# Single-chunk loads of an expert's second weight into three buffers, and no format conversion in the steps that empty the accumulators

## The chip, the cores and the metric

One core of a Trainium2 chip runs the kernel. The metric is device time in microseconds (us) of one execution, lower being better. The kernel before was run three times: 1201.28, 1201.47 and 1202.61 us, with a median of 1201.47 us.

## The reference, cut to what matters

Attention goes first: 32 packed queries `p` per head attend over `k` and `v`, then the 576 queries `q` attend over that packed result. Its output, 2304 tokens of 512, goes through a mixture of four experts, and that through one wide layer with a rational activation.

```python
p_packed = sm_attn(p, k, v)
x = sm_attn(q, p_packed, p_packed)          # 2304 x 512
for e in range(4):                          # experts: w1[e] 512x1024, w2[e] 1024x512
    h = np.maximum(x @ w1[e], 0.0)
    out += p[:, e:e + 1] * (h @ w2[e])
h = out @ w_in                              # 512x2048
g = (a0 + a1*h + a2*h*h + a3*h*h*h) / (1 + |b0|*|h| + |b1|*h*h + 1e-6)
return g @ w_out                            # 2048x512
```

`w_in` and `w_out` arrive as float64; the kernel turns them into float32 pairs on the chip.

## The kernel before, in words

Every float32 product is made of three products of reduced-precision parts: a high part (a rounded copy) and a low part (value minus high part). The copy is made by ACT, the subtraction by POOL or DVE. So each operand of TensorE (PE) costs an ACT and a POOL instruction as well.

**Units and steps.** The work of the experts is a list `units` (line 430): four experts `e`, four batches `bb`, two halves `a_` of the batch's tokens (288 each), eight chunks `c` of 128 of the 1024 inner columns, 256 units in all (`NUM`). The loop at line 674 takes one step `kk` per unit. In step kk PE computes the first product of unit kk (`emit_h`, line 497, six matmuls of 288 columns, the tile `h`). DVE makes `hw` from it (line 507: relu, times the token's weight `pw`), ACT its high part `hh` (508), POOL its low part `hl` (509). Then PE computes the second product of an earlier unit (`emit_out`, line 579, twelve matmuls into four banks of `acc`); it runs two units behind (`lag`, line 656). With chunk 7 a half is complete, and `emit_acc` empties its four banks: ACT copies them for the first expert (614), DVE adds them to the running sum for the others (616). The next half's chunk 0 starts the banks anew, one step later. With kk counted modulo 8, chunk 7's second product and the emptying stand in the steps where it is 1, and the next chunk 0 in those where it is 2.

**Hand-over from one expert to the next.** The second weight's eight chunks stand split in eight slots of `wp` (tile `w`). When the last half of expert e has used chunk c, `refill` (659) calls `put_w2(e + 1, c)` (119) one step later: ACT copies the chunk from the raw buffer into the slot (122), POOL subtracts (123). That is eight steps in a row, c = 0 to 7, in steps that are 3, 4, 5, 6, 7, 0, 1, 2 modulo 8, and there are three hand-overs, e = 0 to 1, 1 to 2, 2 to 3. Expert 0's chunks are put during the start (lines 415, 416, 463). The raw chunks are loaded by `load_raw2` (114): 512 KB, two chunks, into one buffer `r2`. After the odd chunk, `put_w2` issues the load of the next two (125). The load is on SP's queue, whose instructions go out in order. It waits until POOL has read both chunks of the old pair.

**Format conversion.** `narrowing` (160) is a generator that converts `w_in` and `w_out` in 32 tasks. One task takes seven calls of `next(cvt)`: a load (174), four calls with two DVE instructions each (192 and 193, 196 and 197, 199 and 201, 203 and 204), one call with the split (ACT 210, POOL 211), and one with two stores (214). So four of seven calls carry DVE work. Two buffers alternate. The loop makes one call in an even step and two in an odd one (714), from step 40 on. At step 208 it makes what calls are left (680).

**Order inside a step**, as issued, on every engine: first product and its `hw`, `hh`, `hl`; side work (attention for later batches; in two steps of each 16, blocks of the combined first weight, lines 146, 148 and 135); conversion calls; `put_w2`; second product; emptying of the banks. Each engine and SP's queue run their instructions in that order.

Of the kernel before, what the change touches and what calls it, by code (L numbers as in the profile page):

```python
# [8 lines left out]
F32 = mybir.dt.float32  # L9
# [10 lines left out]
def kernel(ctx, tc, q, k, v, p, probs, w1, w2, w_in, a, b, w_out, out):  # L20
    nc = tc.nc
    B, H, S, D = q.shape
    NT, E = probs.shape
    DM = w1.shape[1]
    F1 = w1.shape[2]
    F2 = w_in.shape[1]
    P = 128
# [12 lines left out]
    NCH1 = F1 // P  # L40
# [11 lines left out]
    rawp = moe.enter_context(tc.tile_pool(name="rawp", bufs=1, side="right"))  # L52
    pwp = moe.enter_context(tc.tile_pool(name="pwp", bufs=2, side="right"))

    def f32(ap):
        return ap.bitcast(F32)

    with tc.manual_schedule():
# [47 lines left out]
        raw2 = {}  # L106
# [3 lines left out]
        def load_raw1(e, fh):  # L110
            raw1[fh] = tl = rawp.tile([P, KC, FH], F32, tag=f"r1{fh}", name="r1")
            nc.sync.dma_start(out=tl, in_=w1[e][:, fh * FH:(fh + 1) * FH].rearrange("(k p) f -> p k f", p=P))

        def load_raw2(e, c):
            if e < E:
                raw2[0] = tl = rawp.tile([P, 2, DM], F32, tag="r2", name="r2")
                nc.sync.dma_start(out=tl, in_=w2[e][c * P:(c + 2) * P, :].rearrange("(k p) f -> p k f", p=P))

        def put_w2(e, c):
            w = wts[e, c] = wp.tile([P, 2, DM], F32R, tag="w", name="w")  # L120
            r = raw2[0][:, c % 2, :]
            nc.scalar.activation(out=w[:, 0, :], in_=r, func=AF.Copy)  # L122
            nc.gpsimd.tensor_tensor(out=w[:, 1, :], in0=r, in1=f32(w[:, 0, :]), op=ALU.subtract)  # L123
            if c % 2 == 1:
                load_raw2(*((e, c + 1) if c + 1 < NCH1 else (e + 1, 0)))

        def put_final(n, j):
            w = wts["f", n, j] = wp.tile([P, 2, DM], F32R, tag="w", name="w")
# [204 lines left out]
        def st_s2(i):  # L333
            d = st[i]
            ps = bank2("s2")
            scores(ps, bd[:, i, :], d["qT"])
            t2 = ap1.tile([P, NBLK, 32], F32, tag="t2", name="t2", bufs=2)
            for hf in range(2):
                nc.vector.transpose(
                    out=t2[:, hf * (NBLK // 2):(hf + 1) * (NBLK // 2), :].rearrange("p a n -> p (a n)"),  # L340
                    in_=ps[:, hf, :HALF])
            d["t2"] = t2
# [48 lines left out]
        st_s1(1)  # L391
        st_ppt(0)
        st_s2(0)
        load_raw2(0, 0)
        load_raw1(0, 1)
        st_tr(1, "qr", 0)
        st_tr(1, "qr", 1)
# [124 lines left out]
        def emit_mid(u):  # L522
            if u[0] == "m":
                return
            m, s, c1, c0 = mid[u]
            emit_c1(u)
            nc.vector.scalar_tensor_tensor(out=m, in0=s, scalar=b_abs[:, 1:2], in1=m, op0=ALU.mult, op1=ALU.add)  # L527
            nc.vector.reciprocal(out=m, in_=m)  # L528

        def emit_end(u):  # L530
            if u[0] == "m":
                return
            m, s, c1, c0 = mid[u]
            hh = hp.tile([P, TOK], F32R, tag="hh", name="hh")
            nc.gpsimd.tensor_tensor(out=m, in0=m, in1=c1, op=ALU.mult)  # L535
            nc.scalar.copy(out=hh, in_=m)  # L536
            hs[u] = (hh, None)

        def emit_c1(u):
            m, s, c1, c0 = mid[u]  # L540
            nc.vector.tensor_tensor(out=c1, in0=s, in1=c1, op=ALU.mult)  # L541
            nc.gpsimd.tensor_tensor(out=c1, in0=c1, in1=c0, op=ALU.add)  # L542

        def emit_low(u):
            if u[0] == "m":
                return
            m = mid.pop(u)[0]
            hh = hs[u][0]
            hl = hp.tile([P, TOK], F32R, tag="hl", name="hl")
            nc.gpsimd.tensor_tensor(out=hl, in0=m, in1=f32(hh), op=ALU.subtract)  # L550
            hs[u] = (hh, hl)

        def emit_last(u, v):

            def tt(o, x, y, op):
                nc.vector.tensor_tensor(out=o, in0=x, in1=y, op=op)

            parts = {}
            for w in (u, v):
                hs[w] = [hp.tile([P, TOK], F32R, tag=nm, name=nm) for nm in ("hh", "hl")]  # L560
                m, s, c1, c0 = mid.pop(w)
                cuts = [slice(0, TOK)] if w == u else [slice(x * P, x * P + P) for x in range(SUB)]
                parts[w] = [[y[:, o] for y in (m, c1, *hs[w])] for o in cuts]
                if w == v:
                    nc.vector.scalar_tensor_tensor(out=m, in0=s, scalar=b_abs[:, 1:2], in1=m, op0=ALU.mult, op1=ALU.add)
                else:
                    tt(m, m, c1, ALU.mult)
                    nc.scalar.copy(out=hs[w][0], in_=m)
            (m, _, hh, hl), = parts[u]
            tt(hl, m, f32(hh), ALU.subtract)  # L570
            for (m, c1, hh, hl) in parts[v]:
                nc.vector.reciprocal(out=m, in_=m)
                tt(m, m, c1, ALU.mult)
                nc.scalar.copy(out=hh, in_=m)  # L574
                tt(hl, m, f32(hh), ALU.subtract)
# [60 lines left out]
        def emit_x2(t, bb, c0, n, o, kc):  # L636
            hi, lo = (x[:, kc:kc + 2, o:o + n] for x in xs[t])
            src = acc[bb][:, kc:kc + 2, c0:c0 + n]
            nc.scalar.copy(out=hi, in_=src)
            nc.gpsimd.tensor_tensor(out=lo, in0=src, in1=f32(hi), op=ALU.subtract)  # L640
# [3 lines left out]
        for t in range(NTILE):  # L644
            r = t * TOK
            while r < (t + 1) * TOK:
                n = min((t + 1) * TOK - r, S - r % S)

                n = min(n, HALF - r % HALF)
# [6 lines left out]
        def lag(n):  # L656
            return 2 if n < NUM - 4 else 3 if n < NUM else LAGF
# [16 lines left out]
        for kk in range(NU + LAGF):  # L674
            if kk == ATT:
                att.close()
                accp2 = ctx.enter_context(tc.tile_pool(name="accp2", bufs=1, reuse_waits="tile"))
                acc += [accp2.tile([P, KC, S], F32, name=f"acc{i}") for i in range(2, B)]
                cvt = narrowing(tail.enter_context(tc.tile_pool(name="cv", bufs=2, reuse_waits="tile")))
            if kk == NUM - 3 * PH:  # L680
                for _ in cvt:
                    pass
                tail.close()
                xp0 = ctx.enter_context(tc.tile_pool(name="xp0", bufs=1, reuse_waits="tile"))
                for t in range(2):
                    xs[t] = [xp0.tile([P, KC, TOK], F32R, name=f"x{nm}{t}") for nm in "HL"]
            if kk == NUM:
                moe.close()
                apt.__exit__(None, None, None)
                ps_y = ctx.enter_context(tc.tile_pool(name="ps_y", bufs=2, space=PSUM, reuse_waits="tile"))  # L690
                tp = ctx.enter_context(tc.tile_pool(name="tp", bufs=3, side="right", reuse_waits="tile"))
                yp = ctx.enter_context(tc.tile_pool(name="yp", bufs=3, side="right", reuse_waits="tile"))
                xp1 = ctx.enter_context(tc.tile_pool(name="xp1", bufs=1, side="right", reuse_waits="tile"))
                for t in range(2, NTILE):
                    xs[t] = [xp1.tile([P, KC, TOK], F32R, name=f"x{nm}{t}") for nm in "HL"]
            two_back = units[kk - 2] if 2 <= kk < NU else ("m",)
            if kk < NU - 2:
                emit_end(two_back)
            if kk < NU:
                emit_h(units[kk])  # L700
            if kk == NU:
                emit_c1(units[-1])
            elif kk >= NU - 2:
                emit_end(two_back)
            for f, args in side.pop((kk, 0), ()):
                f(*args)
            if 1 <= kk < NU:
                emit_mid(units[kk - 1])
            if kk < NU:
                emit_low(two_back)  # L710
            elif kk == NU:
                emit_last(*units[-2:])
            emit_acc()
            for _ in range(2 if kk % 2 else 1):
                next(cvt, None)
            if todo and todo[0][0] <= done_cols[0] and (kk < NUM or kk % 2 == 0) and todo[0][1][0] in xs:
                emit_x2(*todo.pop(0)[1])
            if 1 <= kk <= NU and units[kk - 1][0] == "f":
                refill(units[kk - 1], 0)
            if done > refilled:  # L720
                refill(units[done - 1], 1)
                refilled = done
            while done < NU and done + lag(done) <= kk:
                emit_out(units[done])
                done += 1
                if done <= NUM:
                    emit_acc()
            for f, args in side.pop((kk, 1), ()):
                f(*args)
# [30 lines left out]
```

## Time and profile before

| | |
|---|---|
| median of 3 runs | 1201.47 us |
| profiled execution | 1200.13 us |
| its span, first to last instruction | 1198.4 us |
| PE busy | 1127.1 us (94%) |
| DVE busy | 750.0 us (63%) |
| POOL busy | 625.1 us (52%) |
| ACT busy | 542.1 us (45%) |
| mean granted clock of TensorE | 0.977 |

Busy time is the time in which an engine had an instruction under way. A row of the timeline gives start, duration, engine, line, operation, tiles and a count; in brackets stands how long the engine was idle before it and what it waited for. PE can be busy and still not at its peak, so the pace of the steps says more than the share.

### The profile page before, as it was taken

Reading aid. Unit: us, or ns where it says so; the run is one execution under the profiler, and the core shown is the slowest. Engines: PE = TensorE matmul, PEld = TensorE weight load, DVE = VectorE, ACT = ScalarE, POOL = GpSimd, SP = SyncE. Lnnn points to the kernel's source line nnn. Section 1 sums busy time; section 2 is a strip of 40 time slices with the busy share of each in tenths; the row PEclk is TensorE's granted clock in tenths of the full one; section 3 lists DMA queues with packets and bytes.
Section 4 is the critical chain, followed back from the end, with each engine's and each line's share of the span. In section 5 each row is a group of like instructions: output and inputs, shape, how many; then the busy total and the mean of one; then the engine's idle time right before and its main releaser. Section 6 shows DMA issues by size and latency. Waiting matters only on the chain.

```text
span 1198.4 us, 20491 instructions
## 1 busy us (share of the span) xinstructions
PE 1127.1 (94%) x8081; PEld 1027.5 (86%) x8081; DVE 750.0 (63%) x1052; ACT 542.1 (45%) x1081; POOL 625.1 (52%) x658
## 2 busy tenths in 40 slices
PE   5799999969999979999989999999999999999996
PEld 4478889969999878999979999988998899999995
DVE  2343435646677656676632333287888888889886
ACT  3444433332222222222222322177777877787774
POOL 0553435463444354434363533368787777767773
PEclk8799999989999999999999999999999999999998
DMA  9443214242325233324320000243333633354321
GB/s 250 114 119 85 65 46 145 89 122 94 115 78 184 76 111 111 96 96 150 95 76 6 11 6 11 80 138 131 112 139 106 194 125 122 135 148 157 119 93 53
DMA packets 61391, 125.91 MB, mean 105 GB/s; under 512 B 6768, under 2 KB 28272, under 8 KB 61296
## 3 DMA queue, kind: packets, MB, share of 16 engines
q1 hardware_dynamic: 61296, 124.62, 33.3%
q8 instruction: 63, 1.03, 0.4%
q14 instruction: 32, 0.26, 0.1%
HBM read 103.06 MB, written 21.53 MB: 104 GB/s over the span
## 4 chain that ended last, share of the span: by engine, by line
PE 81%; DVE 5%; POOL 5%; DMA 4%; ACT 2%; issue 2%; SPq 0%; ACTq 0%; DVEq 0%; POOLq 0%
PE acc L579 45%; PE h L497 30%; DMA r<-in_moe_w_dram 3%; PE wb L146 3%; POOL w L123 2%; PE tr L274 2%; POOL hl L509 1%; DMA vr<-in_v_dram 1%; PE s L283 1%; DVE m L528 1%; PE pp L320 1%; DVE hw L507 1%; DVE acc L616 1%; ACT e L296 0%; ACT w L122 0%
## 5 line engine op out<-in xcount | busy, mean ns | idle before, releaser
L579 PE MATMUL acc<-hh,w 128*128 128x288 f32 x2048 | 455.4, 298 | 22.6 <-ACT acc L614 9.0
L509 POOL TENSOR_TENSOR hl<-hw,hh 128x288 fp32r<-128x288 f32 x256 | 210.5, 823 | 367.1 <-ACT hh L508 365.9
L579 PEld LDWEIGHTS acc<-hh,w 128*128 128x128 f32 x2048 | 346.0, 190 | 28.7 <-issue 13.6
L507 DVE SCALAR_TENSOR_TENSOR hw<-h,pw 128x288 f32<-128x288 f32 x256 | 116.6, 456 | 327.6 <-PE h L497 290.8
L579 PE MATMUL acc<-hl,w 128*128 128x288 f32 x1024 | 304.6, 297 | 9.0 <-POOL hl L509 8.9
L508 ACT CAST hh<-hw 128x288 fp32r<-128x288 f32 x256 | 110.5, 432 | 381.9 <-DVE hw L507 381.8
L528 DVE RECIPROCAL m<-m 128x384 f32<-128x384 f32 x95 | 242.6, 2553 | 3.2
L497 PE MATMUL h<-aH,wb 128*128 128x288 f32 x1024 | 219.9, 303 | 5.7 <-DVE wb L135 5.7
L579 PEld LDWEIGHTS acc<-hl,w 128*128 128x128 f32 x1024 | 194.6, 190 | 11.0 <-POOL hl L509 11.0
L497 PE MATMUL h<-xH,w 128*128 128x384 f32 x768 | 197.0, 337 | 3.0 <-DVE m L527 3.0
L497 PEld LDWEIGHTS h<-aH,wb 128*128 128x128 f32 x1024 | 165.0, 191 | 36.5 <-issue 25.7
L579 PE MATMUL acc<-w,hh 128*128 128x512 f32 x576 | 194.9, 393 | 0.2 <-ACT hh L574 0.2
L497 PE MATMUL h<-aL,wb 128*128 128x288 f32 x512 | 152.6, 298 | 0.3 <-POOL aL L372 0.3
L497 PEld LDWEIGHTS h<-xH,w 128*128 128x128 f32 x768 | 140.4, 188 | 13.0 <-DVE m L527 5.4
L535 POOL TENSOR_TENSOR m<-m,c 128x384 f32<-128x384 f32 x94 | 95.8, 1019 | 70.9 <-DVE m L528 70.9
L497 PE MATMUL h<-xL,w 128*128 128x384 f32 x384 | 129.4, 337 | 0.0
L579 PEld LDWEIGHTS acc<-w,hh 128*128 128x128 f32 x576 | 108.1, 188 | 21.5 <-ACT y L622 0.8
L579 PE MATMUL acc<-w,hl 128*128 128x512 f32 x288 | 113.9, 395 | 0.0
L542 POOL TENSOR_TENSOR c<-c,c 128x384 f32<-128x384 f32 x96 | 97.9, 1020 | 6.2 <-DVE c L541 4.1
L550 POOL TENSOR_TENSOR hl<-m,hh 128x384 fp32r<-128x384 f32 x94 | 95.8, 1019 | 8.0 <-ACT hh L536 8.0
L497 PEld LDWEIGHTS h<-aL,wb 128*128 128x128 f32 x512 | 97.6, 191 | 0.7 <-POOL aL L372 0.7
L541 DVE TENSOR_TENSOR c<-h,c 128x384 f32<-128x384 f32 x96 | 52.5, 547 | 51.9 <-ACT h L518 49.2
(92 smaller groups left out, 1264.1 us busy)
## 6 DMA issues: line engine op xcount, KB each, us to landing
w<-nw SPq DMA_DIRECT2D x96, 512.0 KB, 4.2
r<-in_moe_w_dram SPq DMA_DIRECT2D x8, 1024.0 KB, 5.8
r<-in_moe_w_dram SPq DMA_DIRECT2D x16, 512.0 KB, 3.4
raw<-in_moe_w_in_dram SPq DMA_DIRECT2D x16, 512.0 KB, 4.2
raw<-in_moe_w_out_dram SPq DMA_DIRECT2D x16, 512.0 KB, 3.7
nw<-raw SPq DMA_DIRECT2D x32, 256.0 KB, 2.3
nw<-t SPq DMA_DIRECT2D x32, 256.0 KB, 2.8
kr<-in_k_dram SPq DMA_DIRECT2D x8, 576.0 KB, 4.6
```

Of the source, the lines that this page charges most:

```text
L123: nc.gpsimd.tensor_tensor(out=w[:, 1, :], in0=r, in1=f32(w[:, 0, :]), op=ALU.subtract)
L146: nc.tensor.matmul(ps[32 * c:32 * c + 32, g, :], bd[r, 2 * bb + g, 32 * c:32 * c + 32], raw1[fh][r, c, :], start=True, stop=True, tile_pos ...
L497: nc.tensor.matmul(ps[:, :n], w, x, start=(i == 0), stop=(i == len(ops) - 1))
L507: nc.vector.scalar_tensor_tensor(out=hw, in0=ph, scalar=0.0, in1=pw[t], op0=ALU.max, op1=ALU.mult)
L508: nc.scalar.copy(out=hh, in_=hw)
L509: nc.gpsimd.tensor_tensor(out=hl, in0=hw, in1=f32(hh), op=ALU.subtract)
L528: nc.vector.reciprocal(out=m, in_=m)
L535: nc.gpsimd.tensor_tensor(out=m, in0=m, in1=c1, op=ALU.mult)
L541: nc.vector.tensor_tensor(out=c1, in0=s, in1=c1, op=ALU.mult)
L542: nc.gpsimd.tensor_tensor(out=c1, in0=c1, in1=c0, op=ALU.add)
L550: nc.gpsimd.tensor_tensor(out=hl, in0=m, in1=f32(hh), op=ALU.subtract)
L579: nc.tensor.matmul(ps[:, :n], w, x, start=(first and i == 0), stop=(last and i == 2))
```

## The change

`load_raw2` loads one chunk (256 KB) instead of two, into one of three buffers of half the size; it takes a running number n = 8e + c. Three loads are issued at the start. Each `put_w2` of chunk n issues the load of chunk n + 3. The second edit sets how many conversion calls a step makes: none where kk is 1 modulo 8, two in the other odd steps, one in even steps, and two where kk is 4 modulo 8.

```diff
-        def load_raw2(e, c):
-            if e < E:
-                raw2[0] = tl = rawp.tile([P, 2, DM], F32, tag="r2", name="r2")
-                nc.sync.dma_start(out=tl, in_=w2[e][c * P:(c + 2) * P, :].rearrange("(k p) f -> p k f", p=P))
+        def load_raw2(n):
+            if n < E * NCH1:
+                raw2[n] = tl = rawp.tile([P, DM], F32, tag="r2", name="r2", bufs=3)
+                nc.sync.dma_start(out=tl, in_=w2[n // NCH1][n % NCH1 * P:(n % NCH1 + 1) * P, :])
 
         def put_w2(e, c):
+            n = e * NCH1 + c
             w = wts[e, c] = wp.tile([P, 2, DM], F32R, tag="w", name="w")
-            r = raw2[0][:, c % 2, :]
+            r = raw2.pop(n)
             nc.scalar.activation(out=w[:, 0, :], in_=r, func=AF.Copy)
             nc.gpsimd.tensor_tensor(out=w[:, 1, :], in0=r, in1=f32(w[:, 0, :]), op=ALU.subtract)
-            if c % 2 == 1:
-                load_raw2(*((e, c + 1) if c + 1 < NCH1 else (e + 1, 0)))
+            load_raw2(n + 3)
...
-        load_raw2(0, 0)
+        for n in range(3):
+            load_raw2(n)
         load_raw1(0, 1)
...
-            for _ in range(2 if kk % 2 else 1):
+
+            for _ in range(0 if kk % NCH1 == 1 else 2 if kk % 2 else 1 + (kk % NCH1 == 4)):
                 next(cvt, None)
```

## Rows read from the trace of the kernel before

**Rows 1.** Waits of PE over the span: us in total, times, longest us.

```profile
PE acc L579 <- ACT acc L614: 9.0, 1, 9.0
PE acc L579 <- DVE acc L616: 8.9, 9, 1.8
PE acc L579 <- POOL hl L509: 8.9, 8, 1.4
```

**Rows 2.** Busy time by engine in two stretches of 16 steps.

```profile
core 0: us, PE busy (x) PEld busy (x) DVE busy (x) ACT busy (x) POOL busy (x), PEclk, DMA share, GB/s
332.88:373.30 40.42, 40.42 (x328) 38.42 (x320) 27.30 (x51) 11.09 (x22) 18.22 (x20) 1.00 0.40 125
687.98:728.40 40.42, 40.42 (x328) 38.42 (x320) 12.61 (x26) 9.37 (x19) 14.20 (x18) 1.00 0.03 8
```

**Rows 3.** Timeline of PE: first matmul of six steps, all at the same place modulo 16.

```profile
238.25 0.40 PE L497 MATMUL h<-aH,wb 128*128 128x288 f32 x1
...
290.29 0.40 PE L497 MATMUL h<-aH,wb 128*128 128x288 f32 x1
...
416.77 0.40 PE L497 MATMUL h<-aH,wb 128*128 128x288 f32 x1
...
470.85 0.40 PE L497 MATMUL h<-aH,wb 128*128 128x288 f32 x1
...
597.12 0.40 PE L497 MATMUL h<-aH,wb 128*128 128x288 f32 x1
...
647.55 0.40 PE L497 MATMUL h<-aH,wb 128*128 128x288 f32 x1
```

**Rows 4.** Chain that ended last, 244 to 268 us: start, us, what.

```profile
252.66 3.44 DMA r<-in_moe_w_dram
...
256.18 0.64 ACT w L122
...
256.89 1.27 POOL w L123
...
260.15 4.14 DMA r<-in_moe_w_dram
```

**Rows 5.** Timeline of PE at the end of the first hand-over.

```profile
265.34 0.61 PE L579 MATMUL acc<-hh,w 128*128 128x288 f32 x1 [9.02 <-ACT acc L614]
```

**Rows 6.** Timeline at one emptying of the banks by DVE.

```profile
391.58 0.69 DVE L204 TENSOR_TENSOR u<-u,t 128x512 f32<-128x512 f32 x1
392.19 1.18 DVE L616 TENSOR_TENSOR acc<-acc,acc 128x288 f32<-128x288 f32 x3
```

**Rows 7.** Timeline of an undisturbed step and the start of the next.

```profile
240.73 0.43 PE L497 MATMUL h<-aH,wb 128*128 128x288 f32 x2
...
242.80 1.09 POOL L509 TENSOR_TENSOR hl<-hw,hh 128x288 fp32r<-128x288 f32 x1 [0.33 <-ACT hh L508]
...
243.11 0.43 PE L497 MATMUL h<-aH,wb 128*128 128x288 f32 x2
```

**Rows 8.** DMA issues: KB each, median us from issue to landing.

```profile
nw<-raw SPq DMA_DIRECT2D x32, 256.0 KB, 2.3
```

**Rows 9.** Groups by line on POOL: busy us, mean ns, idle before.

```profile
L509 POOL TENSOR_TENSOR hl<-hw,hh 128x288 fp32r<-128x288 f32 x256 | 210.5, 823 | 367.1 <-ACT hh L508 365.9 <-DMA nw<-raw 0.5
...
L123 POOL TENSOR_TENSOR w<-r,w 128x512 fp32r<-128x512 f32 x32 | 41.9, 1313 | 32.7 <-ACT w L122 32.7
```

**Rows 10.** Timeline of POOL and DVE early in the second hand-over.

```profile
421.76 1.29 POOL L211 TENSOR_TENSOR t<-u,raw 128x512 fp32r<-128x512 f32 x1 [2.02 <-ACT raw L210]
...
423.07 1.52 DVE L192 TENSOR_SCALAR u<-raw 128x512 int32<-128x512 int32 x1
...
425.21 1.47 POOL L123 TENSOR_TENSOR w<-r,w 128x512 fp32r<-128x512 f32 x1
```

**Rows 11.** Timeline at the start: the first weight blocks, on PE and ACT.

```profile
32.94 1.10 PE L146 MATMUL wb<-r,bd 64*32 64x512 f32 x8
...
36.66 0.99 ACT L148 CAST wb<-wb 128x1024 fp32r<-128x1024 f32 x1
```

**Rows 12.** Waits of SP's queue: us in total, times, longest us.

```profile
SPq L117 <- POOL w L123: 69.0, 15, 11.9
```

## The prediction

> **What bounds the kernel now.** The table shows PE busy for 94% of the span, so I first asked what PE waits for. The list of waits [rows 1] names three that touch this change, and each is some 9 us: once for ACT's copy out of the banks, nine times for DVE's emptying of the banks, eight times for POOL's low part `hl`. A wait understates its harm (the engine starts up again, and the clock may have gone down), so I priced by the pace of the steps.
>
> The pace of undisturbed work comes from two stretches of 16 steps without a hand-over [rows 2]: 40.42 us with format conversions running and 40.42 us without. So conversions cost PE nothing there. Against this stand the stretches between first matmuls at the same place modulo 16 [rows 3]. The three hand-overs lie in 238.25 to 290.29, 416.77 to 470.85 and 597.12 to 647.55: 52.04, 54.08 and 50.43 us, that is 11.6, 13.7 and 10.0 us too long, 35.3 us together. The two stretches between them hold 48 steps each and take 126.48 and 126.27 us against 121.26, so 5.2 and 5.0 us too long, 10.2 us together; the drain waits of [rows 1] are what lies in them. All that this change can give back is these 45.5 us, since before 238 us and after 648 us PE shows no wait for an emptying, and no hand-over lies there.
>
> What makes a hand-over long is seen in the chain [rows 4]: a load of two chunks takes 3.44 us, ACT's copy 0.64, POOL's two subtractions (1.27 for one) with a unit's `hl` between them the rest, and only then does the next load go out, 7.49 us after the last one, that is 3.75 us per chunk. PE frees a slot each step, and a step is 2.38 us [rows 7]. The load is late, and ACT, in order, stands in its queue at the copy of a chunk that hasn't landed; behind it wait `hh` of the current units and, at the end of the first hand-over, the emptying of the banks, for which PE sits idle for 9.02 us [rows 5]. That the weights themselves are not yet due is no help: it is ACT's queue that is blocked.
>
> What makes a drain long is seen in one row pair [rows 6]: conversion work (the last piece 0.69 us) stands ahead of the four additions in DVE's queue, in the very step in which PE needs the banks next.
>
> **The change part by part.**
>
> *Chunk loads, three buffers.* At a hand-over's start three chunks lie ready. Load n + 3 goes out when POOL has done with chunk n, and is wanted three steps, 7.1 us, later. A 256 KB transfer landed in 2.3 us [rows 8] (that is a store; a load of 512 KB took 3.44 to 4.14 [rows 4]). Even with 4.14 us and the 1.9 us of copy and subtraction it is there 1 us early. So ACT's wait for the landing goes. What is late next is POOL. In the eight steps of a hand-over it has eight `hl` of 0.823 us and eight subtractions of 1.313 [rows 9], 17.1 us, and one or two splits of 1.29 us [rows 10] from the conversions: 18.4 to 19.7 us, against 8 x 2.38 = 19.0 us of PE. POOL may lag: `hl` of the step at 240.73 ended at 243.89, and it is read after 245.49, the start of the step after next [rows 7], so 1.6 us are free. By the mean rows nothing is left over. With every instruction at its disturbed length (1.47 for the subtraction [rows 10], 1.09 for `hl` [rows 7]) POOL needs 20.5 + 2.6 = 23.1 us, and 2.5 us per hand-over stay. The means already hold the disturbances as they came, so I keep 1 us each, 3.0 in all, between 0 and 7.5. Gain 32.3 us.
>
> *SP's queue.* It gets 16 more issues and 16 more waits for POOL. Behind a waiting load stand the row `pw` for the half after this one (due eight steps later), conversion loads and stores, and loads of the first weight, due a phase later. A wait ends within the chunk's own step, and nothing behind it is due sooner than that. Cost 0; if the cover were gone, it is the rival on the slower side.
>
> *The start.* 768 KB instead of 512 KB go out ahead of the second half of expert 0's first weight. Half of a 3.44 us load [rows 4] bounds the delay: 0 to 1.7 us. The blocks made of that weight are multiplied from 32.94 us, and ACT copies them at 36.66 [rows 11], as it is busy with other work; most of the delay is hidden there. I take 0.3.
>
> *Conversions moved.* Steps that are 1 modulo 8 lose two calls, steps that are 4 gain one: 11 calls in eight steps instead of 12. From step 40 to 208 there are 21 such rounds, 231 calls, and 1 + 32 x 7 = 225 are needed; so the work is still done in time, about 14 steps later than before, and step 208 finds none to catch up. Each call takes along its loads, stores, ACT copy and POOL split; they keep their order. In the emptying step DVE now has `hw` and the additions alone, and the drains go. A last piece from the call in the step before (two operations of 0.69 [rows 6]) can still stand ahead, but a step earlier. I keep 0.7 of 10.2 us, between 0 and 3. Gain 9.5 us.
>
> What the moved calls could cost: steps 3, 4, 5 modulo 8 now make two calls each. The conversions' DVE time is 27.30 - 12.61 = 14.7 us in 24 calls [rows 2], so a whole task of seven is 4.3 us. Six calls hold at most that, and the `hw` and the block subtraction beside them are 12.61 us in 16 steps, 2.4 us in three. 6.7 us in 7.1 us: no lag, cost 0, and lag of 1.6 us is free besides.
>
> *Sum.* 1200.13 - 32.3 + 0.3 - 9.5 = 1158.6 us for the profiled execution. This lies 1.3 us under the median of the runs, 1201.47, so I forecast **1159.9 us**.
>
> **The rivals.** 0.2% of this time, 2.4 us, is about what a measurement of this kernel can tell from no change.
>
> *Half of the hand-over stays* (0.14). POOL and DVE get in each other's way: a DVE conversion took 1.52 us while POOL subtracted [rows 10]. The Trainium skill ("SBUF — State Buffer", "Who interferes with whom") says that such pairs exclude each other for a whole instruction, whichever starts first; the trace agrees, with that 1.52 us. With POOL full for 19 us, DVE is slowed all through, `hw` and so `hh` come late, and ACT's order passes it on. For it: POOL stands at the edge by the sum above. Against: in the stretch with conversions [rows 2] DVE was busy for 27.30 of 40.42 us, with room left. Price: half of 35.3, 17.6 us instead of 3.0, which gives 1174.5 us.
>
> *The drains stay in part* (0.07): the call in the step before, or the one at 0 modulo 8, runs over. Half of 10.2 us stays, and the time is 1159.9 + 4.4 = 1164.3 us.
>
> *The loads come one at a time* (0.03), the slower side. SP's order decides: if something ahead of load n + 3 holds SP for more than three steps, 7.1 us, after the buffer is free, the third buffer gives nothing, and a chunk takes 3.44 + 0.64 + 1.27 us and 0.15 of hops, 5.5 us, where the pair took 3.75 per chunk. The five chunks after the first three then take 27.5 us against three pairs' 22.5: 5 us more in each hand-over, 15 in all, so 1201.5 + 15 - 9.5 = 1207 us. For it: SP stood 11.9 us in one wait for POOL [rows 12]. Against: that wait was for the very subtraction that frees the buffer, and ends with it. The Trainium skill ("DMA: Bandwidth & Descriptors", "Rules for kernel authors") speaks against transfers this small and wants 1 MiB or more in each. From its fit ("Anatomy of one DMA", about 2.0 us and the bytes over 436 GB/s, for another issuing path) a chunk is, as an estimate, 2.6 us, a serial chunk 4.7, and this rival's end 1195 us. The row's 2.3 us [rows 8] is near that fit.
>
> *All of it* comes back (0.10): 1200.13 - 45.5 + 1.3 = 1156 us. That the edit does not do what it says I give no share of its own: the buffers are three tiles and the calls are counted above.
>
> **How the numbers follow.** My forecast, POOL keeping up with small waits, has 0.66; its own range by the bounds above (0 to 7.5 and 0 to 3 us kept, 0 to 1.7 for the start) is 1156 to 1168. Range: from 1154, the rival that gets all less a measurement's doubt, to 1173, just under half a hand-over kept, which leaves out the serial loads and part of the first rival. Faster by over 0.2%: all cases but the serial loads and what I don't see, 0.95; within: 0.02; slower: 0.03.
>
> **What would show it.** In the changed profile: no idle ACT ahead of line 122 that ends with a landing; PE's wait for ACT's emptying (9.0 us) and for DVE's (8.9 us) gone or under 1 us each; 16 steps around a hand-over at 40.4 to 43 us; the 48 steps between them at 121.3; conversions ending some 14 steps later; POOL busy for nearly all of the eight hand-over steps, and the granted clock at its upper level through them. If PE still waits there for `hl` or `hh` by more than 2.5 us in each, POOL or DVE was sized too small. If ACT still waits for landings, SP's queue was misread. If the emptyings still hold PE, the steps with no call were the wrong ones. A time over 1173 us would make the prediction wrong.

## The result and the profile after

The changed kernel takes 1166.37 us (median of 4 runs, 1164.89 to 1167.37) against 1201.38 us of the kernel before, a ratio of 0.9707 with a 95% interval of 0.969 to 0.9724. That is 35 us less. The forecast was 1159.9 us, about 41.5 us less, in a range of 1154 to 1173. Direction and mechanism held; one term, what stays in the hand-overs, was sized too small.

The waits of PE in the changed kernel, those that answer to [rows 1] (us in total, times, longest us):

```profile
PE acc L580 <- POOL hl L510: 4.8, 5, 1.9
...
PE acc L580 <- ACT acc L615: 2.3, 1, 2.3
```

DVE's emptying, nine waits and 8.9 us before, is no longer in the list. The wait for ACT's emptying fell from 9.0 to 2.3 us, and that for the low part `hl` from 8.9 to 4.8 us.

The busy time by engine in the stretches of the changed kernel that answer to [rows 3] (the first, third and fifth row hold a hand-over and 16 steps, the second and fourth the 48 steps between, the last 16 steps with neither a hand-over nor a conversion):

```profile
core 0: us, PE busy (x) PEld busy (x) DVE busy (x) ACT busy (x) POOL busy (x), PEclk, DMA share, GB/s
240.20:285.48 45.28, 41.06 (x329) 38.54 (x321) 30.78 (x48) 15.89 (x33) 28.65 (x27) 1.00 0.40 123
285.48:406.75 121.27, 121.27 (x968) 115.27 (x960) 86.32 (x154) 32.11 (x64) 52.39 (x58) 1.00 0.32 104
406.75:449.17 42.42, 41.22 (x328) 38.52 (x320) 31.20 (x50) 14.72 (x29) 29.02 (x28) 1.00 0.44 147
449.17:570.45 121.28, 121.28 (x968) 115.28 (x960) 85.51 (x154) 31.56 (x63) 50.71 (x57) 1.00 0.32 107
570.45:613.79 43.34, 41.54 (x328) 38.62 (x320) 34.63 (x52) 14.57 (x29) 29.92 (x27) 1.00 0.28 99
654.22:694.65 40.43, 40.43 (x329) 38.43 (x321) 12.61 (x26) 9.42 (x19) 14.23 (x18) 1.00 0.03 8
```

First column: the 48 steps went from 126.48 and 126.27 us to 121.27 and 121.28, which is the undisturbed pace; all 10.2 us of the emptyings are gone. The hand-overs went from 52.04, 54.08 and 50.43 to 45.28, 42.42 and 43.34 us. Over the pace of 40.43 they keep 4.9, 2.0 and 2.9 us, 9.8 us of 35.3. The granted clock is 1.00, its upper level (2.4 GHz), in all of them. In the kernel before it was not; the three stretches of its hand-overs in the same columns:

```profile
238.25:290.29 52.04, 42.92 (x329) 40.45 (x321) 26.82 (x48) 15.86 (x34) 29.13 (x29) 0.90 0.39 120
416.77:470.85 54.08, 45.55 (x328) 41.33 (x321) 32.77 (x53) 15.04 (x30) 29.47 (x28) 0.94 0.32 111
597.12:647.55 50.43, 44.81 (x329) 41.29 (x321) 17.46 (x32) 13.38 (x27) 24.45 (x25) 0.93 0.15 48
```

Of the 35.3 us there, PE stood idle for 23.3; the other 12.0 are its own work, which took 133.3 us instead of 3 x 40.43 at mean clocks of 0.90 to 0.94. In the changed kernel the 9.8 us are 7.2 of idle time and 2.5 of longer work. So the gain in the hand-overs is about 16 us of waiting and 9.5 us of PE working faster, mostly at the clock that it now keeps.

The sum fits the spans: 35.3 + 10.2 - 9.8 = 35.7 us gained there, of which the start of this execution took back 1.9 (step 59 starts at 240.20 instead of 238.25 us), against 1198.4 - 1164.9 = 33.5 us.

What stays is seen in the timeline of the first hand-over, all engines but PE's undisturbed matmuls:

```profile
243.14 1.48 POOL L124 TENSOR_TENSOR w<-r,w 128x512 fp32r<-128x512 f32 x1
243.39 1.51 DVE L197 TENSOR_SCALAR t<-raw 128x512 int32<-128x512 int32 x1
...
246.49 0.44 ACT L509 CAST hh<-hw 128x288 fp32r<-128x288 f32 x1 [3.67 <-DVE hw L508]
...
247.09 1.27 DVE L204 TENSOR_TENSOR u<-u,t 128x512 f32<-128x512 f32 x1
...
248.39 0.63 ACT L210 ACTIVATE raw<-u 128x512 fp32r<-128x512 f32 x1 [1.46 <-DVE u L204]
248.93 0.62 ACT L123 ACTIVATE w<-r 128x512 fp32r<-128x512 f32 x1
...
252.79 0.40 PE L580 MATMUL acc<-hl,w 128*128 128x288 f32 x1 [1.88 <-POOL hl L510]
```

A conversion operation on DVE takes 1.51 us while POOL subtracts a chunk for 1.48. DVE falls behind, ACT stands 3.67 us for `hw`, then 1.46 for the conversion's split; the chunk copy of line 123 comes late, POOL late after it, and PE waits 1.88 us for `hl`. This is no lack of POOL's time, as PE's list alone would suggest: POOL waits too. The second half of what stays in this hand-over is on SP's queue (same view):

```profile
252.43 0.38 SPq L214 DMA_DIRECT2D nw<-raw  x1
...
255.81 0.33 SPq L174 DMA_DIRECT2D raw<-in_moe_w_out_dram  x1
256.23 3.14 SPq L117 DMA_DIRECT2D r<-in_moe_w_dram  x3
...
260.55 0.63 ACT L123 ACTIVATE w<-r 128x512 fp32r<-128x512 f32 x1 [1.84 <-DMA r<-in_moe_w_dram]
...
262.05 1.28 ACT L615 COPY acc<-acc 128x288 f32<-128x288 f32 x4
```

The conversion's next load (174) waits for the store (214) to land before its buffer is free. The chunk loads (117) stand behind it; three go out together once it has gone. ACT waits for a landing once more, with the copies out of the banks behind it, and that is PE's 2.3 us, against 1.9 for `hl`.

### The profile page after: what moved, and what is told of

Same layout as the page of the kernel before. It is cut to its first block, busy times and chain, and to the rows that moved or that the text cites. A ratio compares the mean times of both kernels' runs of the same rounds, so it can differ in the third digit from the quotient of the medians.

```text
span 1164.9 us, 20530 instructions
## 1 busy us (share of the span) xinstructions
PE 1117.0 (96%) x8081; PEld 1020.3 (88%) x8081; DVE 763.2 (66%) x1052; ACT 543.3 (47%) x1081; POOL 631.6 (54%) x658
## 4 chain that ended last, share of the span: by engine, by line
PE 85%; DVE 4%; POOL 3%; issue 3%; ACT 3%; DMA 2%; SPq 0%; ACTq 0%; POOLq 0%; DVEq 0%
PE acc L580 47%; PE h L498 32%; PE wb L146 3%; PE tr L274 2%; POOL w L124 1%; DMA vr<-in_v_dram 1%; PE s L283 1%; POOL hl L510 1%; DVE m L529 1%; PE pp L320 1%; ACT e L296 1%; PE e1t L308 0%; DMA kr<-in_k_dram 0%; POOL m L536 0%; DVE mx L291 0%
## 5 line engine op out<-in xcount | busy, mean ns | idle before, releaser
L580 PE MATMUL acc<-hh,w 128*128 128x288 f32 x2048 | 449.4, 295 | 2.3 <-ACT acc L615 2.3
L510 POOL TENSOR_TENSOR hl<-hw,hh 128x288 fp32r<-128x288 f32 x256 | 214.2, 838 | 350.1 <-ACT hh L509 349.7
L580 PEld LDWEIGHTS acc<-hh,w 128*128 128x128 f32 x2048 | 342.0, 188 | 5.7 <-issue 2.8
```

What stands on the lines that cost most here:

```text
L510: nc.gpsimd.tensor_tensor(out=hl, in0=hw, in1=f32(hh), op=ALU.subtract)
L580: nc.tensor.matmul(ps[:, :n], w, x, start=(first and i == 0), stop=(last and i == 2))
```

## The experiments

"Kept" is the time of the three 16-step stretches around the hand-overs over the pace, 3 x 40.43 us, from the first matmuls at the same place modulo 16; "clock" is the mean granted clock in each of the three. Both come from one profiled execution of each kernel, while the four times of a kernel lie up to 5.5 us apart (e6, 1164.72 to 1170.22 us), so 1 or 2 us more or less kept say nothing. The ratio is to the kernel before on the same chip; the medians are of several chips. E12 and e13 leave out a part of the result and serve the argument alone.

| run | three stretches, us | clock | kept, us | median, us | ratio, 95% interval |
|---|---|---|---|---|---|
| before | 52.04, 54.08, 50.43 | 0.90, 0.94, 0.93 | 35.3 | 1201.38 | |
| changed | 45.28, 42.42, 43.34 | 1.00, 1.00, 1.00 | 9.8 | 1166.37 | 0.9707 (0.969 to 0.9724) |
| e1 loads only | 41.18, 43.65, 41.04 | 1.00, 1.00, 1.00 | 4.6 | 1172.35 | 0.9746 (0.9727 to 0.9764) |
| e2 calls only | 57.20, 49.08, 52.66 | 0.88, 0.97, 0.97 | 37.7 | 1193.81 | 0.9928 (0.9912 to 0.9944) |
| e3 no calls in hand-over | 40.43, 40.42, 40.43 | 1.00, 1.00, 1.00 | 0 | 1155.41 | 0.961 (0.9595 to 0.9625) |
| e5 two buffers | 51.49, 47.73, 43.94 | 0.93, 0.96, 1.00 | 21.9 | 1176.92 | 0.9783 (0.9762 to 0.9804) |
| e6 split's subtraction on DVE | 45.99, 41.75, 46.18 | 0.96, 1.00, 0.96 | 12.6 | 1169.75 | 0.9734 (0.9712 to 0.9756) |
| e7 added call at 6 | 43.66, 42.45, 44.57 | 1.00, 1.00, 1.00 | 9.4 | 1166.03 | 0.971 (0.9696 to 0.9725) |
| e8 calls late in round | 46.62, 42.11, 42.86 | 0.93, 1.00, 1.00 | 10.3 | 1166.94 | 0.9718 (0.9702 to 0.9735) |
| e9 split's copy on DVE | 45.11, 42.98, 43.69 | 1.00, 1.00, 1.00 | 10.5 | 1167.07 | 0.9695 (0.9672 to 0.9717) |
| e11 whole split on DVE | 46.43, 41.80, 43.44 | 0.96, 1.00, 1.00 | 10.4 | 1165.56 | 0.9685 (0.966 to 0.9709) |
| e10 no split in hand-over | 40.54, 40.43, 40.43 | 1.00, 1.00, 1.00 | 0.1 | 1158.32 | 0.9622 (0.9596 to 0.9647) |
| e12 no chunk subtraction on POOL | 47.52, 40.42, 40.43 | 0.93, 1.00, 1.00 | 7.1 | 1162.92 | 0.966 (0.9644 to 0.9676) |
| e13 e12 with a third raw buffer | 42.88, 40.43, 40.42 | 1.00, 1.00, 1.00 | 2.4 | 1159.59 | 0.9657 (0.9624 to 0.9689) |

**The two edits apart, e1 and e2.** In e1 the loop of calls is as before:

```diff
-            for _ in range(0 if kk % NCH1 == 1 else 2 if kk % 2 else 1 + (kk % NCH1 == 4)):
+            for _ in range(2 if kk % 2 else 1):
```

> The chunk loads with three buffers alone; the conversion calls as before. Theory (the two edits act on different stalls): the hand-overs shrink as in the changed kernel (16 steps around each at 42 to 46 us, where the pace is 40.42 and before had 50 to 54), and the nine waits for DVE's emptying stay at about 9 us, so about 1176.5 us (10 us over the changed kernel). Rival (the calls bunched in steps 3, 4 and 5 modulo 8 are what is left in the hand-overs): the drains cost the same 10 us but the hand-overs go to 41 us each, so about 1169 us.

E2 is the kernel before with the new loop of calls and nothing else.

> The conversion calls of the changed kernel alone; pair loads into one buffer as before. Theory: the waits for DVE's emptying go to 0 and the 48 steps between hand-overs to 121.3 us, the hand-overs stay at 50 to 54 us in 16 steps, so about 1191 us. Rival (what is emptied in time is only seen because the loads run ahead): the drain waits stay in part and the time is over 1195 us.

The waits of PE in e1, with the loads alone:

```profile
PE acc L580 <- DVE acc L617: 8.9, 9, 1.8
...
PE acc L580 <- POOL hl L510: 1.5, 3, 1.0
```

The nine emptyings stand as they were, and of the hand-overs 4.6 us are kept, one emptying wait of 0.6 us among them: less than in the changed kernel. Between the theory (9.8 kept) and the rival (about 2) it lies nearer the rival. The loads alone are worth 30.5 us by the ratio. The waits of PE in e2, with the calls alone, and its 48 steps between hand-overs:

```profile
PE acc L579 <- POOL hl L509: 12.6, 10, 1.9
PE acc L579 <- ACT acc L614: 8.0, 1, 8.0
```

```profile
296.67:417.95 121.28, 121.28 (x969) 115.28 (x961) 86.26 (x154) 31.99 (x64) 52.36 (x58) 1.00 0.32 104
467.03:588.31 121.28, 121.28 (x968) 115.28 (x960) 84.72 (x154) 31.47 (x63) 50.87 (x57) 1.00 0.33 107
```

The emptyings are free here too, whatever the loads do: the second edit alone gives 10.2 us between the hand-overs and keeps 2.4 more in them, 8.6 us less in all by the ratio. Put on top of the loads it gives only 4.7 us (0.9746 to 0.9707), as it raises what the hand-overs keep from 4.6 to 9.8 us. So the edits meet in the hand-overs. One reason is plain in the third of them: conversions fall 14 steps behind, and it then holds 12 conversion operations of DVE, where in e1 it holds 6 and keeps 0.6 us. Their number is not the whole price: the second hand-over holds 12 in both, and e1 keeps 3.2 us of it, the changed kernel 2.0. In the first, e1 keeps 0.7 us against 4.9, with 11 of them against 14, and SP's queue differs too: from 239 to 275 us conversion loads wait for stores for 1.0 us in e1 and for 5.3 us in the changed kernel.

**How far the load runs ahead, e5.**

```diff
-                raw2[n] = tl = rawp.tile([P, DM], F32, tag="r2", name="r2", bufs=3)
+                raw2[n] = tl = rawp.tile([P, DM], F32, tag="r2", name="r2", bufs=2)
...
-            load_raw2(n + 3)
+            load_raw2(n + 2)
...
-        for n in range(3):
+        for n in range(2):
```

> The changed kernel with two chunk buffers instead of three, the memory of the kernel before. Theory (how far the load runs ahead decides): load n + 2 is wanted 4.8 us later and takes 2.6 us, copy and subtraction 1.9 more, 4.5 us in all, so it is just in time while POOL is on time and late when it isn't; ACT waits for landings by some us in each hand-over and the time is 1170 to 1180 us. Rival (single chunks are what matters, two buffers do as well): within 2 us of the changed kernel. Rival (any wait of ACT for a landing costs what it did before): the hand-overs are near 50 us in 16 steps and the time is about 1190 us.

1176.92 us, inside the theory's range. ACT's waits for landings of chunks, in the kernel before, in e5 and in the changed kernel (one line from each list of waits):

```profile
ACT w L122 <- DMA r<-in_moe_w_dram: 43.2, 8, 7.2
```

```profile
ACT w L123 <- DMA r<-in_moe_w_dram: 27.9, 8, 4.6
```

```profile
ACT w L123 <- DMA r<-in_moe_w_dram: 10.2, 6, 4.3
```

With the memory of the kernel before, single chunks in two buffers, with the new calls, already bring 26 of the 35 us; the third buffer takes ACT's wait from 27.9 to 10.2 us and brings the other 9.

**No conversions in the hand-overs, e3.**

```diff
-            for _ in range(0 if kk % NCH1 == 1 else 2 if kk % 2 else 1 + (kk % NCH1 == 4)):
+            for _ in range(0 if kk % NCH1 == 1 or (kk - 59) % 64 < 8 else 2):
```

> The changed kernel, with no conversion call in the eight steps of a hand-over either, and two in every other step. Theory (what is left of the hand-overs, 9.8 us, comes of DVE's conversions and POOL's subtractions holding each other up): 16 steps around a hand-over take 40.4 to 41 us, and the time is about 1157 us. Rival (POOL is full with eight low parts and eight subtractions alone): 16 steps stay at 42 us or more and the time is over 1163 us. Rival (the calls pressed into the other steps bring the drains or new waits back): the 48 steps between take over 123 us.

The stretches of e3 around the hand-overs, and from the first to the end of the last with all between:

```profile
238.68:279.11 40.43, 40.43 (x329) 38.43 (x321) 20.94 (x39) 15.43 (x32) 25.64 (x26) 1.00 0.36 112
400.39:440.81 40.42, 40.42 (x328) 38.42 (x320) 22.43 (x43) 14.23 (x28) 25.68 (x26) 1.00 0.36 113
562.09:602.52 40.43, 40.43 (x328) 38.43 (x321) 12.60 (x26) 13.23 (x26) 22.89 (x24) 1.00 0.14 41
238.68:642.95 404.27, 404.27 (x3209) 384.28 (x3201) 262.06 (x477) 120.46 (x243) 206.19 (x219) 1.00 0.33 103
```

160 steps at the undisturbed pace: PE has no idle time left there. POOL alone, with eight low parts and eight subtractions, is not too full, and two calls in each other step cost nothing (in the third hand-over the conversions had ended: the last split starts at 556.08 us). This version, at 1155.41 us, beats both kernels. But it takes out DVE's, ACT's, POOL's and SP's share of the conversions at once, so it does not say which of them hurts.

**Where the calls stand, e7 and e8.** E7 puts the added call at 6 instead of 4 modulo 8; e8 places the calls by a table:

```diff
-            for _ in range(0 if kk % NCH1 == 1 else 2 if kk % 2 else 1 + (kk % NCH1 == 4)):
+            for _ in range((2, 0, 2, 1, 1, 1, 2, 2)[kk % NCH1]):
```

> The changed kernel with the added conversion call in steps that are 6 modulo 8 instead of 4; as many calls in a hand-over as before. Theory (what is left comes of six calls bunched in the first three steps of a hand-over): the hand-overs keep 2 to 5 us over the pace in all, as with the old order of calls, the emptyings stay free, and the time is about 1160 us. Rival (the number of calls in a hand-over decides, not their order): they keep 8 to 11 us, about 1166 us.

> The changed kernel with 11 calls in eight steps placed as 1, 1, 1, 2, 2, 2, 0, 2 for steps that are 3, 4, 5, 6, 7, 0, 1, 2 modulo 8: few at the start of a hand-over, two in the step just ahead of the emptying. Theory (bunching at the start decides; an emptying is held only by calls in its own step): the hand-overs keep under 4 us, no wait of PE for DVE's emptying over 0.3 us, about 1158 to 1160 us. Rival (calls in the step ahead of the emptying still stand before it): such waits come back, 3 to 10 us in all, 1163 to 1169 us. Rival (a later bunch costs as much as an early one): the hand-overs keep 8 us or more.

Both theories fell: 9.4 and 10.3 us are kept, as in the changed kernel. The bunch in steps 3, 4 and 5 is not the cause, and a bunch elsewhere costs about as much. (Of the 6.2 us that e8's first stretch keeps, 2.6 come of PE's own work, 43.62 us at a mean clock of 0.93 against 41.06 at 1.00 in the changed kernel.) In e8 no wait for DVE's emptying came back, though two calls stand in the step ahead of it.

**The split, e6, e9, e11 and e10.** In the hand-overs so far with three chunk buffers and calls in them, those with two splits had kept 2.4 to 6.2 us and those with one 0.6 to 2.0. So the split was moved: e6 puts its subtraction on DVE, e9 its rounded copy, e11 both.

```diff
-                nc.scalar.activation(out=wh, in_=f32(u), func=AF.Copy)
-                nc.gpsimd.tensor_tensor(out=wl, in0=f32(u), in1=f32(wh), op=ALU.subtract)
+                nc.vector.tensor_copy(out=wh, in_=f32(u))
+                nc.vector.tensor_tensor(out=wl, in0=f32(u), in1=f32(wh), op=ALU.subtract)
```

> The changed kernel with the conversions' subtraction (1.29 us each, one or two in a hand-over) on DVE instead of POOL, everywhere. Theory (in the hand-overs POOL and DVE hold each other up, and DVE falls behind): POOL is relieved, DVE is burdened, and the three hand-overs keep as much as in the changed kernel or more, 8 to 16 us over the pace in all; about 1165 to 1172 us. Rival (POOL has simply 1.3 to 2.6 us too much to do in eight steps): they keep under 4 us, and the time is about 1160 us.

> The changed kernel with the rounded copy of each conversion's split on DVE instead of ACT. So far hand-overs with two splits in them kept 2.4 to 6.2 us, with one 0.6 to 2.0, with none 0. Theory (ACT's queue stands at the split's copy, which waits for DVE, and the chunk copies and high parts stand behind it): hand-overs with two splits go under 2 us, all three keep 2 to 4 us, about 1159 us. Rival (POOL now stands at the split's subtraction, which still waits for DVE): they keep 8 us or more, about 1166 us.

> The changed kernel with both instructions of each split on DVE, so that neither ACT nor POOL has a conversion instruction in its queue. Theory (ACT and POOL waiting at the split for DVE is what is left): all three hand-overs keep under 4 us, about 1158 to 1160 us. Rival (DVE itself, held up by POOL's subtractions, is late with the relu and weight of the next units): they keep 8 us or more, 1165 us and up, and PE's waits are for high parts or for the first product's banks.

They keep 12.6, 10.5 and 10.4 us. In e6 the theory held; in e9 and e11 the rival did. With no conversion instruction in ACT's or POOL's queue, e11 keeps as much as the changed kernel, so it is not ACT or POOL standing at a split. (In e11's first stretch 1.9 us more than in the changed kernel's are PE's own work, 42.96 us at a mean clock of 0.96.) Why two splits go with more kept than one stays open: the second and third hand-over of the changed kernel both hold 12 conversion operations, with one split and with two. The third hand-over of e11 shows the one engine that is late:

```profile
587.45 1.74 POOL L124 TENSOR_TENSOR w<-r,w 128x512 fp32r<-128x512 f32 x1
588.07 1.67 DVE L204 TENSOR_TENSOR u<-u,t 128x512 f32<-128x512 f32 x1
589.66 0.45 DVE L508 SCALAR_TENSOR_TENSOR hw<-h,pw 128x288 f32<-128x288 f32 x1
...
590.14 0.43 ACT L509 CAST hh<-hw 128x288 fp32r<-128x288 f32 x1 [4.60 <-DVE hw L508]
```

A DVE operation of 0.69 us [rows 6] takes 1.67 beside POOL's subtraction, and POOL's takes 1.74 against its mean of 1.31 [rows 9]; ACT stands idle for 4.60 us until DVE gets to `hw`.

E10 puts the split off to after the hand-over and leaves the DVE calls:

```diff
+                if not (at_split and (kk - 59) % 64 < 8):
+                    at_split = next(cvt, None) == "split next"
```

> The changed kernel, in which a conversion call that would make a split is put off to after the hand-over, with its DVE calls (up to one task's, four calls) still made in it; two calls in every other step but the emptying one. Theory (the splits are what hurts): the hand-overs keep under 1 us in all, about 1156 to 1157 us. Rival (DVE's conversion work itself hurts, being slowed and slowing POOL): with half of that work left, half of the 9.8 us is kept, 4 to 5 us, about 1160 us.

It keeps 0.1 us, but this does not tell the two apart: a put-off split holds back what follows it too, and only 4, 2 and 0 conversion operations of DVE were left in its hand-overs.

**POOL's subtraction out of the way, e12.**

```diff
-            nc.gpsimd.tensor_tensor(out=w[:, 1, :], in0=r, in1=f32(w[:, 0, :]), op=ALU.subtract)
+            nc.scalar.activation(out=w[:, 1, :], in_=r, func=AF.Copy)
```

> The changed kernel without POOL's subtraction of a chunk: the low part of the second expert weight is left out and a second rounded copy of the chunk, by ACT, put in its place. The conversion calls stay where they are. Theory (POOL's subtractions and DVE's conversions stretch each other): the conversion operations in a hand-over take near their undisturbed length (14 of them some 8 us instead of 14.3), PE does not wait, 16 steps take 40.4 to 41 us and the time is 1156 to 1158 us. Rival (the number of DVE operations in a hand-over is too much by itself): 8 us or more are kept, 1165 us.

The second and third hand-over go to 40.42 and 40.43 us with every conversion call in its place; the first keeps 7.1 us, so the time, 1162.92 us, lies between the theory's and the rival's. The 14 conversion operations of the first take 10.3 us, not the 8 of the theory. For the second one, its eight steps in the changed kernel and in e12 hold the same 25 instructions on DVE:

```profile
406.75:427.86 21.11, 19.91 (x152) 19.21 (x145) 16.70 (x25) 8.63 (x17) 15.86 (x15) 1.00 0.36 123
```

```profile
409.37:428.39 19.02, 19.02 (x152) 19.02 (x145) 12.56 (x25) 12.27 (x24) 7.95 (x10) 1.00 0.47 150
```

16.70 us in the one and 12.56 in the other: the 4.1 us of difference are DVE standing behind POOL. ACT's waits for landings, 3.1 and 3.0 us, are still there in these two hand-overs, and cost PE nothing. So the hold of POOL and DVE on each other is shown for two of three hand-overs, 4.9 of the 9.8 us. In the first one it has a part as well: in e7 ACT has no wait for a landing there, and 3.2 us are kept. POOL itself was busy for 15.86 us of 21.11 in the changed kernel; it had 5 us to spare and was late all the same. The Trainium skill ("SBUF — State Buffer", "Who interferes with whom") states that a DVE operation with two SBUF inputs, or in a two-port mode, and a POOL operation that reads SBUF exclude each other for the whole instruction. The trace agrees: in the second hand-over line 203, an operation with two inputs, ends 0.55 us after the subtraction that it met in the changed kernel, and takes 0.69 us in e12 (the last row).

```profile
415.78 1.48 POOL L124 TENSOR_TENSOR w<-r,w 128x512 fp32r<-128x512 f32 x1
416.14 1.67 DVE L203 SCALAR_TENSOR_TENSOR t<-raw,t 128x512 f32<-128x512 uint32 x1
...
417.50 0.69 DVE L203 SCALAR_TENSOR_TENSOR t<-raw,t 128x512 f32<-128x512 uint32 x1
```

An operation on line 197, with one input, takes 0.41 us in e12's first hand-over and 1.51 in the changed kernel's; whether it ran in a two-port mode no run here shows.

The first hand-over of e12 shows the second part without POOL's subtractions, on SP's queue and ACT's. It is larger there than in the changed kernel (PE waits 4.17 us for the emptying instead of 2.3), and ACT makes one more copy for each chunk:

```profile
253.16 0.33 SPq L174 DMA_DIRECT2D raw<-in_moe_w_out_dram  x1
253.58 2.37 SPq L117 DMA_DIRECT2D r<-in_moe_w_dram  x3
...
259.57 0.63 ACT L123 ACTIVATE w<-r 128x512 fp32r<-128x512 f32 x1 [4.43 <-DMA r<-in_moe_w_dram]
...
262.43 0.61 PE L580 MATMUL acc<-hh,w 128*128 128x288 f32 x1 [4.17 <-ACT acc L615]
```

A conversion load that waits for a store to land lets the chunk loads go at 253.58 only, and the first lands 5.9 us later, with the 512 KB of that load ahead of it.

**SP's queue freed, e13**, on top of e12:

```diff
-                raw = raws[n] = cv.tile([P, N, 2], I32, tag="raw", name="raw")
+                raw = raws[n] = cv.tile([P, N, 2], I32, tag="raw", name="raw", bufs=3)
```

> The kernel of the run before (the low part of the second expert weight left out, a rounded copy by ACT in its place) with a third buffer for the conversions' raw input, so that their next load does not wait on SP's queue for a store that has just gone out. In the run before the first hand-over kept 7.1 us and the others 0. Theory (chunk loads stood on SP's queue behind a conversion load that waited 3 us for its store to land, and then shared the transfers with it): the first hand-over keeps under 1.5 us, and the time is 1156 to 1158 us. Rival (SP's order has no part in it, ACT's waits come of the copies' own order): 7 us stay, 1163 us.

The same place in e13:

```profile
250.05 0.46 SPq L174 DMA_DIRECT2D raw<-in_moe_w_out_dram  x1
...
250.61 2.63 SPq L117 DMA_DIRECT2D r<-in_moe_w_dram  x3
...
256.72 0.63 ACT L123 ACTIVATE w<-r 128x512 fp32r<-128x512 f32 x1 [2.22 <-DMA r<-in_moe_w_dram]
```

The loads go out at 250.61 instead of 253.58, and the first hand-over keeps 2.4 us instead of 7.1. The stretch in e12 and in e13:

```profile
240.57:288.09 47.52, 43.35 (x329) 41.12 (x321) 26.49 (x48) 19.79 (x41) 17.00 (x19) 0.93 0.38 117
```

```profile
239.92:282.80 42.88, 40.69 (x328) 38.46 (x320) 27.32 (x48) 19.86 (x41) 16.90 (x19) 1.00 0.43 130
```

Of the 4.6 us between them 2.0 are idle time of PE and 2.7 its own work, at a mean clock of 0.93 in e12. So SP's order had a part, as the theory had it, but neither the stretch (under 1.5 us kept) nor the time (1156 to 1158 us, measured 1159.59) went as far as it named. By their medians, on one chip, e13 is 3.3 us faster than e12; by their ratios to the kernel before, 0.9657 and 0.966, the two can't be told apart, so the gain of the third buffer rests on this one stretch and the medians. The first of the three still lands 6.0 us after its issue, beside two stores and a 512 KB load that went out just ahead. That the rest is the shared transfers was not tried by itself.

## Why the prediction was right or wrong

- *What bounds the kernel* held. The two stalls, priced by the pace of the steps, were 35.3 and 10.2 us, and e3 gives back all 45.5 of them in its 160 steps at full pace. That pricing from stretches was worth more than the list of waits, which had 9 us for each: 12.0 of the 35.3 us were PE's own longer work and not a wait. The list named three waits and left out a fourth in the hand-overs, four times for ACT's `hh`, 4.7 us, which is gone too.
- *Chunk loads.* The gain was put at 32.3 us. Alone they bring 30.5 us (e1), so that term was sound by itself. The sentence that the load is there 1 us early was not: ACT still waits for landings for 10.2 us in six waits.
- *SP's queue, cost 0*, was wrong in its reason. It said that nothing behind a waiting chunk load is due sooner, and missed the other way round: a chunk load behind a conversion load that waits for a store. The rival on the slower side had that mechanism and asked for a delay of 7.1 us; e12 shows 3 us of it, in one hand-over of three, and in the changed kernel PE waited 2.3 us there.
- *Conversions moved.* The gain of 9.5 us was right in place and nearly in size: all 10.2 us went, alone (e2) and together. The work ends 14 steps later, as counted (its last split starts at 618.79 instead of 607.15 us).
- *The step that failed* is "No lag, cost 0" with the 3.0 us kept (0 to 7.5): 9.8 us were kept, 4.9 of them in the two hand-overs where e12 shows the cause. The DVE time of the conversions, 4.3 us a task, was taken from a stretch without a hand-over [rows 2]. In a hand-over POOL's subtractions stretch the same instructions from 12.56 to 16.70 us (e12 against the changed kernel). The row for it was there, 1.52 us for one operation [rows 10], and was given to a rival instead of to the term. The 9.8 us lie outside the 0 to 7.5; that the time was in the range all the same is owed to its width and not to this term. The 7.5 us of the bound came from POOL's sum alone, but POOL was not full; it waited for ACT, and ACT for DVE.
- *The rivals.* "Half of the hand-over stays" named the right mechanism and twice the size: 9.8 us instead of 17.6. "The drains stay in part" did not happen, in any of the runs with no call in the emptying step; neither did "all of it", which e3 then reached.
- *The start*, 0.3 us, can't be told. Step 59 began at 240.20 us in the changed kernel, at 239.47 in e2 with the old loads and at 238.59 in e7 with the new ones; landings at the start vary by more than the term.
- *Signs named beforehand.* Between the hand-overs 121.3 us, the granted clock and the end of the conversions came as said. The waits of ACT for landings and of PE for ACT's emptying (2.3 us against under 1), two of three stretches over 43 us, and a POOL that is not nearly full did not.

## What to carry to other kernels

A load that feeds an in-order engine should run so far ahead that the engine never waits for it, since what can hurt is the work queued behind the wait; three small buffers did here what one large one couldn't, at half a buffer's more memory. Price background work from the stretch in which it will run, with the neighbours that it will have there, not from a quiet one. And where two engines hold each other up, taking the background work out of the few steps that need both beats spreading it evenly.

## What the runs showed that was not expected

POOL and DVE stretch each other while neither is near full: 25 equal DVE instructions took 16.70 us beside POOL's chunk subtractions and 12.56 without them.

The same emptying wait of 1.80 us came once with the granted clock at its upper level throughout and once with a fall after it. The same two steps, the wait in the first, in the kernel before and in e1:

```profile
390.04:396.81 6.77, 4.97 (x38) 4.77 (x37) 4.45 (x9) 1.40 (x3) 2.66 (x4) 1.00 0.11 39
```

```profile
380.31:388.63 8.32, 6.52 (x39) 6.32 (x37) 4.45 (x9) 1.40 (x3) 3.23 (x4) 0.79 0.18 64
```

PE was idle for 1.80 us in both (6.77 - 4.97 and 8.32 - 6.52); at a mean granted clock of 0.79 instead of 1.00 its work takes 1.55 us longer. What decides whether a wait of that length costs the clock was not tried.
